# DCN-v2 cross layers on Trainium2: the first layer's second half column-tiled, both halves' remainder products in one place

## The chip, the cores and the metric

The kernel runs on one core of one Trainium2 chip. The metric is the device time of one execution in microseconds (us), as the median of several runs. PE is the matrix engine, and PEld its weight loads; DVE, ACT, POOL and SP are the vector, scalar, general-purpose and sync engines. SP and ACT also issue transfers (DMA).

## What is computed

```python
B, F, D, L = 4096, 26, 16, 6
Din = min(F * D, 1024)                 # 416
x0: (B, Din) bf16, ws: (L, Din, Din) bf16, bs: (L, Din) bf16
def reference(x0, ws, bs):
    x = x0
    for l in range(ws.shape[0]):
        x = x0 * (x @ ws[l] + bs[l]) + x
    return x
```

Six cross layers, one after the other, over 4096 rows of 416 features.

## The kernel before

The state is kept transposed: features on partitions, batch rows along the free dimension. 416 features are 3 chunks of 128 (`NK`, index k for the input features and m for the output features) and a remainder of 32 (`R`). The batch is 2 halves (`NS`, index s) of 4 groups (`NG`, index g) of 512 columns (`CW`). `XM[0]` holds x0, and `XM[1]`, `XM[2]` the running state, alternately. The 32 remainder features of the four groups stand side by side on the partitions of `XR`: group g of half s on partitions 32g to 32g+31, columns 512s on. `XRd` is a copy of `XR[0]` with the upper and lower 64 partitions exchanged; the first layer's row products for m = 1 read it, on the other two strips of the array than those for m = 0 and 2.

For each output chunk m and two groups (a "block": one half s, one pair of groups h, two banks of PSUM) PE makes:

- full products: 3 chunks k of 128 features by 512 columns for each group. In the first layer (`full` in `first_layer`, L214) a product uses the whole 128x128 array. In the later layers (`mm_full`, L181) it is cut into four, column-tiled: 32 output features each, side by side in the array.
- row products (L221 in the first layer, L187 in `mm_row`): the 32 remainder features as input, row-tiled, 32 rows of the array for each group.
- remainder products (`mm_rem`, L193 and L198): the 32 remainder features as output, column-tiled, one strip for each group; 16 instructions for a half.

ACT evicts a block from PSUM with the bias added (`ew_main`, L165), DVE multiplies by x0 (L166) and adds the state (L169). `ew_rem` does the same for a half's remainder (L173, L174, L175).

The first layer runs while x0 comes in. SP issues the transposing transfers of x0 (`load_x0t`, L76) in the order (s,g) = (0,0), (0,1), (0,2), (0,3), (1,0); then the second half's remainder columns (`load_xrem1`, L85); then (1,1), (1,2), (1,3), and after them the weights of the later layers (L72, L91) and the rows of x0 (L125). The second half's remainder comes as plain rows into `xrem`; POOL copies it to `xrig` (L134), PE transposes it (`x0_rem`, L157) and DVE copies the result from PSUM into `XR[0]` and `XRd` (L160). For the first half `xrig` is loaded directly.

`first_layer(s)` handles one half: the blocks of groups 0 and 1 for m = 0, 1, 2 (`pa`), the row products that close them and open the fourth block, then the three blocks of groups 2 and 3 (`pb`), their last row products, and then the half's remainder products into `pr`. In the first half the transposes of `x0_rem(1)` follow, into the second part of the same tile `pr`. Then the eviction of the remainder. From the second layer on (the loop over l up to LL-1) `rem_pair` makes both halves' remainder products together, once a layer, behind the first two output chunks. The last layer is done by rows (L327, L333, L336), with the results leaving from DVE's sums (L344, L355).

All PSUM tiles come from one pool of four buffers of two banks; a tile takes the buffer that was given back first, and PE waits until it was evicted. Each engine works through its instructions in order.

Of the kernel before, what the change touches and what calls it, by code (L numbers as in the profile page):

```python
# [11 lines left out]
BF16 = mybir.dt.bfloat16  # L12
FP32 = mybir.dt.float32
# [3 lines left out]
def kernel(  # L17
# [7 lines left out]
    nc = tc.nc  # L25
    B, D = x0.shape
    L = ws.shape[0]
    P = 128
# [3 lines left out]
    NS = 2  # L32
    NG = 4
    CW = 512
# [8 lines left out]
    psum = ctx.enter_context(tc.tile_pool(name="psum", bufs=4, space=bass.MemoryType.PSUM))  # L43
# [4 lines left out]
    ident = const.tile([P, P], BF16)  # L48
# [12 lines left out]
    scrR = [big.tile([P, 4, P], BF16, name=f"scrR{s}") for s in range(NS)]  # L61
    xrem = big.tile([P, 16, R], BF16)
    xrig = big.tile([P, NS, 4, P], BF16)
# [4 lines left out]
    def col0(s, g):  # L68
        return SW * s + CW * g
# [84 lines left out]

    def x0_rem(s, tpr):
        for i in range(4):
            nc.tensor.transpose(tpr[:, 128 * i:128 * i + 128], xrig[:, s, i, :], ident[:])  # L157
        for dst, src in ((slice(0, P), slice(0, P)), (slice(64, P), slice(0, 64)), (slice(0, 64), slice(64, P))):
            to = XR[0] if dst == src else XRd
            nc.vector.tensor_copy(to[dst, CW * s:CW * s + CW], tpr[src])  # L160

    def ew_main(l, s, m, h, pt, cur, nxt, pin=False):
        c0 = col0(s, 2 * h)
        t = tpool.tile([P, 2 * CW], BF16, name="t")
        nc.scalar.activation(t[:], pt[:].rearrange("p a b -> p (a b)"), ACT.Identity, bias=bM[:, m, l:l + 1], scale=1.0)  # L165
        prod = nc.vector.tensor_tensor(out=t[:], in0=t[:], in1=XM[0][:, m, c0:c0 + 2 * CW], op=ALU.mult)  # L166
        if pin:
            tc.keep_in_program_order(prod)
        nc.vector.tensor_tensor(out=nxt[:, m, c0:c0 + 2 * CW], in0=t[:], in1=cur[:, m, c0:c0 + 2 * CW], op=ALU.add)  # L169

    def ew_rem(l, s, pr, curR, nxtR):
        tr = tpool.tile([P, 2 * CW], BF16, name="t")
        nc.scalar.activation(tr[:, 0:CW], pr, ACT.Identity, bias=bR[:, l:l + 1], scale=1.0)  # L173
        nc.vector.tensor_tensor(out=tr[:, 0:CW], in0=tr[:, 0:CW], in1=XR[0][:, CW * s:CW * s + CW], op=ALU.mult)  # L174
        nc.vector.tensor_tensor(out=nxtR[:, CW * s:CW * s + CW], in0=tr[:, 0:CW], in1=curR[:, CW * s:CW * s + CW], op=ALU.add)  # L175

    def mm_full(l, s, m, g, pts, cur, first, last):
        c0 = col0(s, g)
        for k in range(NK):
            for q in range(4):  # L180
                nc.tensor.matmul(pts[g // 2][32 * q:32 * q + 32, g % 2, :], lhsT=WM[:, l, k, 128 * m + 32 * q:128 * m + 32 * q + 32],  # L181
                                 rhs=cur[:, k, c0:c0 + CW], start=(first and k == 0), stop=(last and k == NK - 1),
                                 tile_position=(0, 32 * q))
# [7 lines left out]
    def mm_rem(l, s, pr, cur, curR):  # L191
        for g in range(NG):
            nc.tensor.matmul(pr[32 * g:32 * g + 32, :], lhsT=WD[:, l, g, :], rhs=curR[:, CW * s:CW * s + CW],  # L193
                             start=True, stop=False, tile_position=(0, 32 * g))
        for k in range(NK):
            for g in range(NG):
                c0 = col0(s, g)
                nc.tensor.matmul(pr[32 * g:32 * g + 32, :], lhsT=WM[:, l, k, NK * P:D], rhs=cur[:, k, c0:c0 + CW],  # L198
                      start=False, stop=(k == NK - 1), tile_position=(0, 32 * g))
# [4 lines left out]
    def xl_dmat(s, k, nxt):  # L204
        nc.sync.dma_start_transpose(out=XLrows[:, 16 * s:16 * s + 16, 128 * k:128 * k + 128],
                                    in_=nxt[:, k, SW * s:SW * s + SW])

    def first_layer(s):
        cur, curR, nxt, nxtR = XM[0], XR[0], XM[1], XR[1]

        def full(pt, m, h, gl, after_row):
            c0 = col0(s, 2 * h + gl)
            for k in range(NK):
                nc.tensor.matmul(pt[:, gl, :], lhsT=WM[:, 0, k, 128 * m:128 * m + 128], rhs=cur[:, k, c0:c0 + CW],  # L214
                                 start=(k == 0 and not after_row), stop=(k == NK - 1 and after_row))

        def row(pt, m, h, opens):
            for gl in range(2):
                rg = 32 * ((2 * h + gl) ^ (2 if m == 1 else 0))
                src = XRd if m == 1 else curR  # L220
                nc.tensor.matmul(pt[:, gl, :], lhsT=WR[rg:rg + 32, 0, 128 * m:128 * m + 128],  # L221
                                 rhs=src[rg:rg + 32, CW * s:CW * s + CW],
                                 start=opens, stop=not opens, tile_position=(rg, 0))

        def ph(m):
            return psum.tile([P, 2, CW], FP32, tag="ps", name=f"ph{m}")

        pa = [ph(m) for m in range(NK)]
        if s == 0:
            for m in range(NK):  # L230
                full(pa[m], m, 0, 0, False)
            tp0 = psum.tile([P, CW], BF16, tag="ps", name="tpr")
            x0_rem(0, tp0[:])
            for m in range(NK):
                full(pa[m], m, 0, 1, False)
        else:
            for m in range(NK):
                for gl in range(2):
                    full(pa[m], m, 0, gl, False)
        pb = [ph(0)]  # L240
        row(pa[0], 0, 0, False)
        row(pb[0], 0, 1, True)
        row(pa[2], 2, 0, False)
        row(pa[1], 1, 0, False)
        for m in range(NK):
            ew_main(0, s, m, 0, pa[m], cur, nxt)
        for m in range(NK):
            if m:
                pb.append(ph(m))
            for gl in range(2):  # L250
                full(pb[m], m, 1, gl, m == 0)
        row(pb[1], 1, 1, False)
        row(pb[2], 2, 1, False)
        pr = psum.tile([P, 2, CW], FP32, tag="ps", name="pr")
        mm_rem(0, s, pr[:, 0, :], cur, curR)
        if s == 0:
            x0_rem(1, pr[:, 1, :].bitcast(BF16)[:, 0:CW])
        for m in range(NK):
            ew_main(0, s, m, 1, pb[m], cur, nxt, pin=(s == 0))
        ew_rem(0, s, pr[:, 0, :], curR, nxtR)  # L260

    bias_setup()
    pe_filler(1, CW)
    for s in range(NS):
        first_layer(s)

    def rem_pair(l, cur, curR, nxtR, feeds_last):
        pr2 = psum.tile([P, 2, CW], FP32, tag="ps", name="pr2")
        for s in range(NS):
            mm_rem(l, s, pr2[:, s, :], cur, curR)  # L270
        for s in range(NS):
            ew_rem(l, s, pr2[:, s, :], curR, nxtR)
            if feeds_last:
                nc.sync.dma_start_transpose(out=scrR[s][:], in_=nxtR[:, CW * s:CW * s + CW])

    def xl_rem(s):
        tc.keep_in_program_order(
# [3 lines left out]
    cur, curR = XM[1], XR[1]  # L281
    for l in range(1, LL):
        nxt, nxtR = XM[1 + (l % 2)], XR[1 + (l % 2)]
        feeds_last = (l == LL - 1)
# [10 lines left out]
        for n in range(0, len(tiles), 2):  # L295
            ta, tb = tiles[n], tiles[n + 1]
            pts[ta] = new_pts()
            for g in range(NG):
                mm_full(l, ta[0], ta[1], g, pts[ta], cur, True, False)
            mm_row(l, ta[0], ta[1], pts[ta], curR, False, True)  # L300
            pts[tb] = new_pts()
            mm_row(l, tb[0], tb[1], pts[tb], curR, True, False)
            if feeds_last and n == 4:
                xl_rem(0)
            finish(ta)
            for g in range(NG):
                mm_full(l, tb[0], tb[1], g, pts[tb], cur, False, True)
            finish(tb)
            if n == 0:
                rem_pair(l, cur, curR, nxtR, feeds_last)  # L310
        if feeds_last:
            xl_rem(1)
        cur, curR = nxt, nxtR

    l = LL
# [97 lines left out]
```

## Time and profile before

| | |
|---|---|
| median of 3 runs | 130.97 us (130.72 to 131.04) |
| the profiled execution | 130.71 us, of which the profile's span is 128.9 us |
| PE busy | 123.1 us (96% of the span), 1,690 products |
| DVE busy | 107.1 us (83%) |
| ACT busy | 86.9 us (67%) |
| POOL busy | 5.9 us (5%) |
| granted PE clock | 0.998 of full speed |

All times in the lines are us from the start of the span, and durations of single instructions on the page are ns. A line of a timeline gives start, length, engine, source line, operation, output and inputs, the shape, and how many instructions are merged in it. `128*32` stands for 128 rows and 32 columns of the array. Each product is listed at 0.38 us because its length includes the pipeline; products follow each other at shorter intervals, so starts are compared with starts. An idle stretch stands in brackets behind the instruction that ends it, with what released it. In the chain that ended last, each piece is what the next one waited for, and a piece of PE is merged from neighbouring instructions of one line.

### The profile page before, as it was taken

To read this page: it belongs to the slowest core of one execution; us is meant where nothing else is said; L and a number is where in the kernel's file an instruction comes from. 1 tells how busy PE (TensorE), PEld (TensorE's weight loads), DVE (VectorE), ACT (ScalarE), POOL (GpSimd) and SP (SyncE) were. 2 spreads that over 40 slices of the span, in tenths; PEclk is the share of its full clock that TensorE was granted. 3 is DMA by queue.
4 is the path that set the end of the run, shared out by engine and by line. 5 is a ranking of instruction groups with operands and counts; after the bars stand their busy time and mean duration, and the time that the engine had idled before them with its cause. 6 is when DMAs were issued, how large, how long until landed. Compare 5 with 4: busy or idle time off the path is not lost.

```text
span 128.9 us, 3973 instructions
## 1 busy us (share of the span) xinstructions
PE 123.1 (96%) x1690; PEld 54.9 (43%) x1690; DVE 107.1 (83%) x197; ACT 86.9 (67%) x99; POOL 5.9 (5%) x18
## 2 busy tenths in 40 slices
PE   6999999999999999999999999999999999999960
PEld 2343443354444444444444444444444445445420
DVE  1032979999999898989898989898989899898991
ACT  0426783987848577848668848668847896569670
POOL 4022200600000000000000000000000000000000
PEclk9999999999999999999999999999999999999999
DMA  3999999999990000000000000000297999995754
GB/s 106 237 203 217 170 158 260 247 328 333 336 299 11 5 0 8 0 0 5 0 5 0 5 0 5 0 5 0 42 166 164 123 219 178 187 323 188 231 179 139
DMA packets 42102, 16.37 MB, mean 127 GB/s; under 512 B 30906, under 2 KB 42084, under 8 KB 42084
## 3 DMA queue, kind: packets, MB, share of 16 engines
q1 hardware_dynamic: 39416, 15.56, 54.6%
q10 hardware_dynamic: 2668, 0.56, 2.3%
q8 instruction: 13, 0.21, 0.7%
q14 instruction: 5, 0.04, 0.1%
HBM read 6.15 MB, written 3.41 MB: 74 GB/s over the span
## 4 chain that ended last, share of the span: by engine, by line
PE 80%; DMA 8%; DVE 5%; issue 2%; SPq 1%; ACT 1%; DVEq 0%
PE pt L181 49%; PE ph L214 9%; DMA XM<-in_x_dram 8%; PE py L327 8%; PE pt L187 5%; PE pr L198 5%; DVE t L355 3%; DVE o L344 2%; PE pr L193 2%; SPq L76 1%; PE py L333 1%; PE ph L221 1%; PE py L336 1%; ACT t L354 1%; PE pr L157 0%
## 5 line engine op out<-in xcount | busy, mean ns | idle before, releaser
L181 PE MATMUL pt<-XM,WM 128*32 128x512 bf16 x1152 | 65.2, 379 | 0.0
L165 ACT ACTIVATE t<-pt,bM 128x1024 bf16<-128x1024 f32 x48 | 49.6, 1115 | 18.3 <-PE pt L187 18.3
L166 DVE TENSOR_TENSOR t<-t,XM 128x1024 bf16<-128x1024 bf16 x60 | 41.4, 690 | 5.3 <-ACT t L165 5.3
L169 DVE TENSOR_TENSOR XM<-t,XM 128x1024 bf16<-128x1024 bf16 x60 | 41.8, 696 | 3.4
L181 PEld LDWEIGHTS <-WM 128*32 128x32 bf16 x1152 | 29.7, 97 | 33.8 <-issue 5.1
L354 ACT CAST t<-py 128x416 bf16<-128x416 f32 (+1 forms) x23 | 14.8, 642 | 4.8 <-PE py L327 2.1
L327 PE MATMUL py<-WM,XM 128*128 128x416 bf16 x96 | 17.7, 340 | 0.0
L214 PE MATMUL ph<-XM,WM 128*128 128x512 bf16 x72 | 16.5, 379 | 0.1
L165 ACT ACTIVATE t<-ph,bM 128x1024 bf16<-128x1024 f32 x12 | 12.5, 1114 | 4.4 <-PE ph L221 4.4
L327 PEld LDWEIGHTS <-XM 128*128 128x128 bf16 x96 | 9.0, 98 | 8.5 <-issue 1.4
L355 DVE TENSOR_TENSOR t<-t,X0rows 128x416 bf16<-128x416 bf16 (+1 forms) x23 | 10.4, 454 | 1.2 <-ACT t L354 1.2
L214 PEld LDWEIGHTS <-WM 128*128 128x128 bf16 x72 | 6.8, 98 | 8.6 <-issue 1.3
L344 DVE TENSOR_TENSOR o<-t,XLrows 128x416 bf16<-128x416 bf16 (+1 forms) x23 | 10.3, 451 | 0.0
L173 ACT ACTIVATE t<-pr,bR 128x512 bf16<-128x512 f32 x10 | 6.4, 684 | 2.7 <-PE pr L198 2.1
L198 PE MATMUL pr<-XM,WM 128*32 128x512 bf16 x120 | 8.2, 379 | 0.0
L187 PE MATMUL pt<-XR,WR 32*128 32x512 bf16 x96 | 7.3, 379 | 0.0
L141 PE MATMUL wps<-warm 128*128 128x512 bf16 (+1 forms) x11 | 4.4, 593 | 1.2 <-DVE warm L94 1.2
L175 DVE TENSOR_TENSOR XR<-t,XR 128x512 bf16<-128x512 bf16 x10 | 4.2, 423 | 0.7
L198 PEld LDWEIGHTS <-WM 128*32 128x32 bf16 x120 | 3.2, 97 | 3.1
L106 ACT ACT_TABLE_LOAD x1 | 1.3, 1283 | 4.3 <-DMA WM<-in_ws_dram 4.3
L174 DVE TENSOR_TENSOR t<-t,XR 128x512 bf16<-128x512 bf16 x10 | 4.2, 418 | 0.0
L152 DVE CAST bM<-pb 128x18 f32<-128x18 bf16 x1 | 0.2, 177 | 4.6 <-PE pb L151 4.6
(39 smaller groups left out, 33.6 us busy)
## 6 DMA issues: line engine op xcount, KB each, us to landing
X0rows<-in_x_dram SPq DMA_DIRECT2D x4, 832.0 KB, 11.6
out_dram<-o SPq DMA_DIRECT2D x9, 208.0 KB, 2.4
WM<-in_ws_dram SPq DMA_DIRECT2D x5, 312.0 KB
out_dram<-o SPq DMA_DIRECT2D x13, 104.0 KB, 1.7
WR<-in_ws_dram SPq DMA_DIRECT2D x4, 130.0 KB, 4.1
WM<-in_ws_dram ACTq DMA_DIRECT2D x1, 312.0 KB
XM<-in_x_dram SPq DMA_TRANSPOSE x8, 4.9
xrig<-in_x_dram ACTq DMA_DIRECT2D x4, 32.0 KB, 4.1
```

The source lines that it names most:

```text
L165: nc.scalar.activation(t[:], pt[:].rearrange("p a b -> p (a b)"), ACT.Identity, bias=bM[:, m, l:l + 1], scale=1.0)
L166: prod = nc.vector.tensor_tensor(out=t[:], in0=t[:], in1=XM[0][:, m, c0:c0 + 2 * CW], op=ALU.mult)
L169: nc.vector.tensor_tensor(out=nxt[:, m, c0:c0 + 2 * CW], in0=t[:], in1=cur[:, m, c0:c0 + 2 * CW], op=ALU.add)
L173: nc.scalar.activation(tr[:, 0:CW], pr, ACT.Identity, bias=bR[:, l:l + 1], scale=1.0)
L181: nc.tensor.matmul(pts[g // 2][32 * q:32 * q + 32, g % 2, :], lhsT=WM[:, l, k, 128 * m + 32 * q:128 * m + 32 * q + 32], rhs=cur[:, k, c0:c ...
L187: nc.tensor.matmul(pts[g // 2][:, g % 2, :], lhsT=WR[32 * g:32 * g + 32, l, 128 * m:128 * m + 128], rhs=curR[32 * g:32 * g + 32, CW * s:CW ...
L198: nc.tensor.matmul(pr[32 * g:32 * g + 32, :], lhsT=WM[:, l, k, NK * P:D], rhs=cur[:, k, c0:c0 + CW], start=False, stop=(k == NK - 1), tile ...
L214: nc.tensor.matmul(pt[:, gl, :], lhsT=WM[:, 0, k, 128 * m:128 * m + 128], rhs=cur[:, k, c0:c0 + CW], start=(k == 0 and not after_row), sto ...
L327: nc.tensor.matmul(py[:, 0:D], lhsT=cur[:, k, q_cols(q, g)], rhs=WM[:, l, k, :], start=((not closes) and k == 0), stop=(closes and k == NK ...
L344: tc.keep_in_program_order(nc.vector.tensor_tensor(out=o, in0=t, in1=xl, op=ALU.add))
L354: nc.scalar.copy(tv, src)
L355: tc.keep_in_program_order(nc.vector.tensor_tensor(out=tv, in0=tv, in1=X0rows[:, b, :], op=ALU.mult))
```

## The change

In the second half of the first layer (s = 1) three things differ:

- `full` calls `mm_full`, so that the 36 full products are 144 column-tiled ones.
- `x0_rem(1)` makes 16 column-tiled transposes of 32 by 128 instead of 4 of 128 by 128, into a tile of its own (`tp1`).
- The remainder products of both halves are made by one call of `rem_pair`, behind the fourth block of the second half (its first block of groups 2 and 3), and their evictions follow there. The first half makes none, and the second half none at its end.

The function `rem_pair` is only moved up in the file, unchanged. The source lines below the edit shift by up to 17 (in the kernel after, `full` stands at L231, the row products at L238, the transposes at L157 and L161, `mm_full` at L186).

```diff
--- before.py
+++ after.py
@@ -154,7 +154,12 @@
 
     def x0_rem(s, tpr):
         for i in range(4):
-            nc.tensor.transpose(tpr[:, 128 * i:128 * i + 128], xrig[:, s, i, :], ident[:])
+            if s == 0:
+                nc.tensor.transpose(tpr[:, 128 * i:128 * i + 128], xrig[:, s, i, :], ident[:])
+                continue
+            for g in range(NG):
+                nc.tensor.transpose(tpr[32 * g:32 * g + 32, 128 * i:128 * i + 128], xrig[:, s, i, 32 * g:32 * g + 32], ident[:],
+                                    tile_position=(0, 32 * g))
         for dst, src in ((slice(0, P), slice(0, P)), (slice(64, P), slice(0, 64)), (slice(0, 64), slice(64, P))):
             to = XR[0] if dst == src else XRd
             nc.vector.tensor_copy(to[dst, CW * s:CW * s + CW], tpr[src])
@@ -205,10 +210,22 @@
         nc.sync.dma_start_transpose(out=XLrows[:, 16 * s:16 * s + 16, 128 * k:128 * k + 128],
                                     in_=nxt[:, k, SW * s:SW * s + SW])
 
+    def rem_pair(l, cur, curR, nxtR, feeds_last):
+        pr2 = psum.tile([P, 2, CW], FP32, tag="ps", name="pr2")
+        for s in range(NS):
+            mm_rem(l, s, pr2[:, s, :], cur, curR)
+        for s in range(NS):
+            ew_rem(l, s, pr2[:, s, :], curR, nxtR)
+            if feeds_last:
+                nc.sync.dma_start_transpose(out=scrR[s][:], in_=nxtR[:, CW * s:CW * s + CW])
+
     def first_layer(s):
         cur, curR, nxt, nxtR = XM[0], XR[0], XM[1], XR[1]
 
         def full(pt, m, h, gl, after_row):
+            if s == 1:
+                mm_full(0, s, m, 2 * h + gl, {h: pt}, cur, not after_row, after_row)
+                return
             c0 = col0(s, 2 * h + gl)
             for k in range(NK):
                 nc.tensor.matmul(pt[:, gl, :], lhsT=WM[:, 0, k, 128 * m:128 * m + 128], rhs=cur[:, k, c0:c0 + CW],
@@ -249,29 +266,20 @@
                 pb.append(ph(m))
             for gl in range(2):
                 full(pb[m], m, 1, gl, m == 0)
+            if s == 1 and m == 0:
+                rem_pair(0, cur, curR, nxtR, False)
         row(pb[1], 1, 1, False)
         row(pb[2], 2, 1, False)
-        pr = psum.tile([P, 2, CW], FP32, tag="ps", name="pr")
-        mm_rem(0, s, pr[:, 0, :], cur, curR)
         if s == 0:
-            x0_rem(1, pr[:, 1, :].bitcast(BF16)[:, 0:CW])
+            tp1 = psum.tile([P, CW], BF16, tag="ps", name="tpr")
+            x0_rem(1, tp1[:])
         for m in range(NK):
             ew_main(0, s, m, 1, pb[m], cur, nxt, pin=(s == 0))
-        ew_rem(0, s, pr[:, 0, :], curR, nxtR)
 
     bias_setup()
     pe_filler(1, CW)
     for s in range(NS):
         first_layer(s)
-
-    def rem_pair(l, cur, curR, nxtR, feeds_last):
-        pr2 = psum.tile([P, 2, CW], FP32, tag="ps", name="pr2")
-        for s in range(NS):
-            mm_rem(l, s, pr2[:, s, :], cur, curR)
-        for s in range(NS):
-            ew_rem(l, s, pr2[:, s, :], curR, nxtR)
-            if feeds_last:
-                nc.sync.dma_start_transpose(out=scrR[s][:], in_=nxtR[:, CW * s:CW * s + CW])
 
     def xl_rem(s):
         tc.keep_in_program_order(
```

## The prediction

> **What bounds the kernel now.** The page comes first: which engine is full, and at what clock.
>
> ```profile
> PE 123.1 (96%) x1690; PEld 54.9 (43%) x1690; DVE 107.1 (83%) x197; ACT 86.9 (67%) x99; POOL 5.9 (5%) x18
> PEclk9999999999999999999999999999999999999999
> ```
>
> PE is nearly always at work and at full clock. The chain that ended last says whether it ever waits:
>
> ```profile
> 12.10 0.04 issue
> 12.14 3.40 PE ph L214 x15
> ...
> 26.25 0.65 PE pr L198 x12
> 26.90 2.59 PE pt L181 x48
> 29.49 0.54 PE pt L187 x8
> 30.03 2.71 PE pt L181 x48
> ```
>
> From 12.14 on, when the last transposed block of the first half has landed, to 115.8, every piece of the chain is PE. So whatever moves the start of the second layer's products (L181) moves the end, unless something else gives way. PE's own timeline gives the starts around the change:
>
> ```profile
> 15.47 0.39 PE L221 MATMUL ph<-XRd,WR 32*128 32x512 bf16 x2
> ...
> 15.80 0.40 PE L193 MATMUL pr<-XR,WD 128*32 128x512 bf16 x4
> 16.02 0.82 PE L198 MATMUL pr<-XM,WM 128*32 128x512 bf16 x12
> 16.78 0.40 PE L157 MATMUL pr<-ident,xrig 128*128 128x128 bf16 x4
> ```
>
> ```profile
> 21.00 0.60 PE L221 MATMUL ph<-XR,WR 32*128 32x512 bf16 x6
> ...
> 21.54 4.06 PE L214 MATMUL ph<-XM,WM 128*128 128x512 bf16 x18
> ...
> 26.73 2.76 PE L181 MATMUL pt<-XM,WM 128*32 128x512 bf16 x48
> 29.42 0.61 PE L187 MATMUL pt<-XR,WR 32*128 32x512 bf16 x8
> ```
>
> The second half's full products start at 17.01. Call u one pass of 512 columns (one full product, or four tiled ones side by side) and s the extra time where the tiling changes. From 17.01 to 21.00 there are 18 passes and a change, 18u+s = 3.99; from 21.00 to 21.54 two and a change, 2u+s = 0.54. So u = 0.216 and s = 0.11 us. The 48 column-tiled products of L181, 12 passes, take 26.73 to 29.42: 12u+s = 2.69 again. A column-tiled pass costs PE what a full one does. Last, what feeds PE here, from POOL's and SP's timelines:
>
> ```profile
> 15.26 0.79 POOL L134 COPY xrig<-xrem 128x512 bf16<-128x512 bf16 x1 [4.76 <-DMA xrem<-in_x_dram]
> ```
>
> ```profile
> 11.45 2.68 SPq L76 DMA_TRANSPOSE XM<-in_x_dram  x1
> ```
>
> That copy feeds the second half's transposes of L157; its semaphore rises at 16.07. The transfer issued at 11.45 is the second half's second block (g=1); in the trace the last of its 16 landing events is at 17.13. Before, PE comes to the transposes at 16.78 and to that block three passes after 17.01, at 17.66: both are ready, by 0.7 and 0.5 us. The first half's four passes of remainder products, 15.80 to 16.66, are what hides them.
>
> **The change, part by part.** *Tiling.* The 36 full products become 144 column-tiled ones and the 4 transposes 16: 120 more pairs of load and product on PE (1,810 for 1,690), in the same number of passes. PE's changes of tiling between 15.80 and L181: before five (products to transposes, full to row, row to full, full to row, row to column); after, counted from the end of the row products at 15.80, four (column to row and back, twice). Gain: one s, 0.11 us.
>
> The loads: by form, the profile has
>
> ```profile
> L181 PEld LDWEIGHTS <-WM 128*32 128x32 bf16 x1152 | 29.7, 97 | 33.8 <-issue 5.1
> L214 PEld LDWEIGHTS <-WM 128*128 128x128 bf16 x72 | 6.8, 98 | 8.6 <-issue 1.3
> ```
>
> 97 and 98 ns, both beside running passes of 216: no cost for the products. The transposes have passes of only 128 columns. Full ones went 56 ns apart, 0.23 for four; no row shows column-tiled ones that short with loads of 32 columns. Bounds: 0.23 if the loads hide, 0.39 if each group of four waits out one load (4 times 97). Nearest is L157 itself, so 0.23; the rest of the sum absorbs either. [...]
>
> *The remainder products of the first half leave 15.80 to 16.66.* They go, with the second half's, behind the fourth block of the second half: 8 passes there for 4+4 before, so no work is saved, and the cover over the copy and the transfer is gone. From the end of the row products, after:
>
> - PE stands ready at 15.80; POOL's copy lets the transposes start at 16.11 (semaphore 16.07 and 0.04, as a load followed its landing at 8.33 by 0.04). They end their passes at 16.34.
> - Three passes on the block g=0 (landed 13.95): 16.98.
> - The block g=1 lands at 17.13; PE resumed 0.04 after the landing at 12.11, so here at 17.17.
> - 15 passes: 20.40. Change, two row passes, change: 21.05.
> - 6 passes of the fourth block, 8 of remainders, 12 of the last two blocks, no change of tiling between: 26u = 5.61, so 26.66.
> - Change, one row pass, change: 27.09, where L181 starts. Before it was 26.73.
>
> So +0.36 us. Without waits the same passes would bring L181 to 26.61 (-0.12: the change of tiling saved, and rounding); the waits at the copy and at the block together add 0.48.
>
> *What is moved past what.* The issue order on SP is unchanged and its transfers wait only for transfers, so the landings stay. ACT no longer has the first half's remainder eviction (0.69 us at L173) and DVE no longer its two operations of 0.42 before the second half; both come after the third block's. The next waits in line after: block g=3 lands at 21.27 and PE comes to it at 21.70. The remainder tile takes the buffer of the half's first block. ACT's row tells when that is empty:
>
> ```profile
> 21.43 4.13 ACT L165 ACTIVATE t<-ph,bM 128x1024 bf16<-128x1024 f32 x4 [2.12 <-PE ph L221]
> ```
>
> It began 0.43 after the row products at 21.00, and one eviction is 1.115 long; after, the row products are at 20.51, so the buffer is free at 22.05, and PE wants it at 22.35. Cover 0.30. The other two blocks' evictions follow 1.0 apart (23.06 and 24.06), wanted at 24.07 and 25.37. DVE needs 1.33 per block and 0.9 per remainder: the remainder rows of the second layer, wanted at 29.8, are written by about 26.9, and the last block of the first layer at about 31.8 (before 31.4), wanted not before 34. So nothing else stands in the way, and +0.36 goes to the end.
>
> The profiled execution took 130.71 in all, around a span of 128.9; it is at the lower end of the runs (130.72 to 131.04, median 130.97). I add to the median: 131.33. A measurement of this kernel can tell about 0.3%, 0.39 us, from no change, so the forecast lies just inside that edge.
>
> **Rivals.** *The waits vanish.* Block g=1 lands by 16.67 and the copy is done by 15.80; then only the tiling change is left: -0.12, 130.85. For it: transposed blocks took 4.9 us to land by the median, this one 5.7; at 4.9 it would be there at 16.36. Against: the copy alone then still holds PE to 16.98 (+0.17), and an earlier queue would also start PE earlier at 12.14, in both kernels. Chance 0.14, with 0.06 in it for a gain above 0.39 of which I see no source: PE's passes are fixed.
>
> *An instruction block falls on the transfer.* In the trace one 16 KB packet of instructions runs from 17.84 to 18.94, and of the 16 landings of block g=2 four come by 18.71 and twelve only at 19.80 to 19.93. With four times the instructions per pass PE may ask for it sooner. It decides if it starts before 17.0: block g=1 then lands up to 1.1 later, near 18.2, and the sum is +1.4: 132.4. Against: in before the packet came 0.7 after the landing at 17.13, which PE's instruction stream waits for after as well, at nearly the same count. Chance 0.10. [...]
>
> *The remainder tile waits for its buffer.* The cover of 0.30 fails if ACT starts the half's evictions later or waits for the second of them (23.06, 0.7 after 22.35). Price 0.1 to 0.7, say 0.4: +0.75, 131.7. Chance 0.10.
>
> **How the numbers follow.** The forecast has 0.66: +0.17 (the copy alone binds) to +0.6 (the landing 0.25 later than profiled). About half of it lies above 0.39, rather more since the unseen costs only add: 0.35 of 0.66. Slower: 0.35+0.10+0.10 = 0.55. Faster 0.06, same the rest, 0.39. The range leaves out the instruction block and the unseen gain: from 130.85 to 132.0, which holds both the vanished waits and most of the buffer case, and the spread of the median.
>
> **What would show it.** After: PE idle before the second half's transposes until about 16.1, released by POOL's copy; a second gap before the 13th column-tiled product of that half, released by the transfer, near 17.17; L181 of the second layer at 27.1; no gap before the remainder products; the remaining 88.9 us to 115.6 unchanged. It is wrong if L181 starts at 26.6, if the gap ends past 17.5, or if PE idles at 22.3.

## The result, and the profile after

The kernel after took 131.87 us (median of 9 runs, 131.58 to 132.99) beside 130.97 before: 0.90 us more, ratio 1.0088 (95% interval 1.0065 to 1.0110). A second job (a later set of runs of both kernels) gave 131.57 beside 130.78, 1.0060 (1.0042 to 1.0077). It is slower, and by over twice the 0.36 us forecast.

No engine that limits the kernel has more work to speak of: PE has its 120 additional pairs of load and product in 0.3 us more of busy time. POOL has 0.9 us more, 0.35 of it in the copy of L134 (1.15 us for 0.79):

```profile
PE 123.4 (95%) x1810; PEld 55.5 (43%) x1810; DVE 107.4 (83%) x197; ACT 86.9 (67%) x99; POOL 6.8 (5%) x18
```

The chain that ended last, in order of time, now leaves PE between 12 and 17 us. Before, it was PE from 12.14 on; here it runs over the remainder's transfer and POOL's copy:

```profile
9.36 1.75 SPq L76
11.11 0.04 issue
11.16 4.53 DMA xrem<-in_x_dram
...
15.80 1.16 POOL xrig L134
16.96 0.04 issue
17.00 0.41 PE tpr L161 x16
17.41 3.88 PE ph L186 x72
21.29 0.54 PE ph L238 x8
21.84 1.41 PE ph L186 x24
```

PE's timeline (the idle time before an instruction and its releaser in brackets at the end) shows the one gap:

```profile
15.63 0.39 PE L238 MATMUL ph<-XR,WR 32*128 32x512 bf16 x2
17.00 0.41 PE L161 MATMUL tpr<-ident,xrig 128*32 128x128 bf16 x16 [0.99 <-POOL xrig L134]
17.23 4.06 PE L186 MATMUL ph<-XM,WM 128*32 128x512 bf16 x72
21.23 0.60 PE L238 MATMUL ph<-XR,WR 32*128 32x512 bf16 x6
...
21.77 1.48 PE L186 MATMUL ph<-XM,WM 128*32 128x512 bf16 x24
...
27.82 2.77 PE L186 MATMUL pt<-XM,WM 128*32 128x512 bf16 x48
```

The transposes could have started at 15.95 (0.33 after the row products); they started at 17.00. The second layer starts at 27.82, 1.09 later than before; from there to the last instruction it is 102.2 us in both. Some of the 1.09 is not the change's: the last block of the first half landed at 12.25 here and 12.11 before. So from here on the time is counted from the first half's last row products (L221 before) to the second layer's first product, written D. Landing times are the last of a transfer's 16 landing events, as in the prediction. Before, D is 26.73 less 15.48, 11.25; after, 27.82 less 15.62, 12.20.

A second and a third profile of the same kernel show the gap in another shape. The third's PE:

```profile
15.74 0.39 PE L238 MATMUL ph<-XR,WR 32*128 32x512 bf16 x2
16.33 0.41 PE L161 MATMUL tpr<-ident,xrig 128*32 128x128 bf16 x16 [0.20 <-POOL xrig L134]
16.56 0.82 PE L186 MATMUL ph<-XM,WM 128*32 128x512 bf16 x12
17.78 3.42 PE L186 MATMUL ph<-XM,WM 128*32 128x512 bf16 x60 [0.40 <-DMA XM<-in_x_dram]
```

Here the copy ends early, and the 13th product waits for block g=1, exactly the two gaps that the prediction drew. (The bracket counts from the end of the listed length; by starts PE lost 17.78-16.56-0.65 = 0.57 there.)

### The profile page after: what moved, and what is told of

It is laid out like the page before. It is cut to its first block, busy times and chain, and to the rows that moved or that the text cites. A ratio compares the mean times of both kernels' runs of the same rounds, so it can differ in the third digit from the quotient of the medians.

```text
span 130.0 us, 4214 instructions
## 1 busy us (share of the span) xinstructions
PE 123.4 (95%) x1810; PEld 55.5 (43%) x1810; DVE 107.4 (83%) x197; ACT 86.9 (67%) x99; POOL 6.8 (5%) x18
## 4 chain that ended last, share of the span: by engine, by line
PE 77%; DMA 7%; DVE 5%; SPq 4%; issue 2%; POOL 1%; ACT 1%; DVEq 0%; POOLq 0%
PE pt L186 49%; PE py L335 8%; PE ph L186 6%; PE pt L192 5%; PE pr L203 5%; SPq L76 4%; DMA XM<-in_x_dram 4%; DMA xrem<-in_x_dram 3%; DVE t L363 3%; DVE o L352 2%; PE pr L198 2%; PE py L341 1%; POOL xrig L134 1%; PE py L344 1%; PE ph L238 1%
## 5 line engine op out<-in xcount | busy, mean ns | idle before, releaser
L186 PE MATMUL pt<-XM,WM 128*32 128x512 bf16 x1152 | 65.2, 379 | 0.0
L186 PEld LDWEIGHTS <-WM 128*32 128x32 bf16 x1296 | 33.4, 97 | 37.6 <-issue 5.7
L231 PE MATMUL ph<-XM,WM 128*128 128x512 bf16 x36 | 8.7, 389 | 0.1
L186 PE MATMUL ph<-XM,WM 128*32 128x512 bf16 x144 | 8.3, 379 | 0.0
L231 PEld LDWEIGHTS <-WM 128*128 128x128 bf16 x36 | 3.4, 100 | 4.6 <-issue 1.3
L203 PEld LDWEIGHTS <-WM 128*32 128x32 bf16 x120 | 3.2, 97 | 3.3
```

## The experiments

Three theories went in. P: the loss is PE's wait for POOL's copy, which the first half's remainder products used to cover. T: the transfer of block g=1 binds right behind it. C, the rival: column-tiled products cost PE more than whole-array ones.

**The move without the tiling.** In the kernel after, the branches for s = 1 are taken out of `x0_rem` and `full`; the cut in `full` is shown:

```diff
-            if s == 1:
-                mm_full(0, s, m, 2 * h + gl, {h: pt}, cur, not after_row, after_row)
-                return
```

> The kernel after without its tiling: the second half's 36 products and 4 transposes use the whole array again, only the remainder products are moved. Theory P (the move took away PE's cover over POOL's copy of the second half's remainder, and PE waits for that copy): the loss stays, with two more changes of tiling around the moved remainder products (0.22 us) on top of the kernel after: 131.9 to 132.2 us, PE idle before the transposes until POOL's copy ends. Theory C (the column-tiled products and transposes cost PE more than the whole-array ones): the loss is gone, 130.9 to 131.2 us.

Measured 131.91 us, ratio 1.0086 (1.0054 to 1.0118). The loss stays although that half's 36 full products and its transposes use the whole array, so C falls. PE's timeline has a third gap, at the fourth block's second group:

```profile
16.11 0.40 PE L158 MATMUL tpr<-ident,xrig 128*128 128x128 bf16 x4 [0.28 <-POOL xrig L134]
16.34 0.81 PE L228 MATMUL ph<-XM,WM 128*128 128x512 bf16 x3
17.44 3.40 PE L228 MATMUL ph<-XM,WM 128*128 128x512 bf16 x15 [0.29 <-DMA XM<-in_x_dram]
...
22.32 0.81 PE L228 MATMUL ph<-XM,WM 128*128 128x512 bf16 x3 [0.19 <-DMA XM<-in_x_dram]
```

By starts these are 0.34, 0.45 and 0.35 us. Block g=3 landed at 22.28; it is the transfer that the prediction named as next in line, with 0.43 of cover from a landing at 21.27.

**The tiling without the move.** The kernel before, with the two tiled branches of the change's diff and nothing else of it.

> The kernel before with only the tiling of the second half's products and transposes; the first half's remainder products stay ahead of the transposes. Theory P: the cover is back, no wait at the transposes, one change of tiling fewer than before: 130.85 us, 0.12 under the kernel before. Theory C: the loss stays, 131.7 to 132.0 us.

> The kernel before with only the tiling, once more for its times: one change of tiling saved, 0.11 to 0.13 us under the kernel before (ratio 0.999).

Measured 130.70 beside 130.83 (ratio 0.9984, 0.9968 to 1.0000), and in the second job 130.85 beside 130.83 (1.0002, 0.9987 to 1.0017). PE does not wait:

```profile
15.72 0.39 PE L229 MATMUL ph<-XR,WR 32*128 32x512 bf16 x2
16.04 0.40 PE L198 MATMUL pr<-XR,WD 128*32 128x512 bf16 x4
...
16.91 0.40 PE L161 MATMUL pr<-ident,xrig 128*32 128x128 bf16 x16
17.14 4.06 PE L186 MATMUL ph<-XM,WM 128*32 128x512 bf16 x72
...
26.87 2.76 PE L186 MATMUL pt<-XM,WM 128*32 128x512 bf16 x48
```

D is 11.15 in both of its profiles, 0.10 under the kernel before: the one change of tiling saved. In the time that is too little to tell from nothing. So no kernel here is shown to beat the kernel before; of the change, the tiling is harmless and the move is the loss.

**The remainder's transfer earlier.** In the kernel after, in SP's order:

```diff
-    load_x0t(1, 0)
     load_xrem1()
+    load_x0t(1, 0)
```

> The kernel after with one transfer earlier in SP's order: the second half's remainder rows go ahead of that half's first block instead of behind it, so POOL's copy is done some 1 to 2 us sooner. Theory P alone: PE no longer waits, 130.85 us. Theory T (as predicted: the block g=1 of the second half is next and binds as well): PE comes to it at about 16.8 and waits until its landing at 17.1 to 17.7, so 131.2 to 131.7 us, with the gap before the 13th tiled product. Theory C: no change from the kernel after, 131.9 us.

Measured 131.46, ratio 1.0044 (1.0025 to 1.0062). The copy ended at 14.30, no gap is left before the transposes, and all of the wait stands before block g=1 (landed 17.42):

```profile
15.94 0.41 PE L161 MATMUL tpr<-ident,xrig 128*32 128x128 bf16 x16
16.18 0.82 PE L186 MATMUL ph<-XM,WM 128*32 128x512 bf16 x12
17.46 3.42 PE L186 MATMUL ph<-XM,WM 128*32 128x512 bf16 x60 [0.47 <-DMA XM<-in_x_dram]
```

P alone would have brought it to 130.85. T holds: with the copy out of the way PE still waits 0.63 us by starts for the transfer alone (D is 11.79, 0.64 over the 11.15 of the tiling alone). The transposes follow the row products at once here, so their new tile `tp1` does not wait for its buffer either.

**Three passes ahead of the transposes.** In the kernel after, `x0_rem(1)` comes behind the first block's group g=0 of the second half (the part of the edit that moves it):

```diff
+            if s == 0 and m == 0:
+                early.append(psum.tile([P, 2, CW], FP32, tag="ps", name="ph0"))
+                mm_full(0, 1, 0, 0, {0: early[0]}, cur, True, False)
+                tp1 = psum.tile([P, CW], BF16, tag="ps", name="tpr")
+                x0_rem(1, tp1[:])
```

> The kernel after with the second half's first three passes (block g=0, landed at about 14) put ahead of the transposes, 0.65 us of cover over POOL's copy. Theory P alone: the loss shrinks by 0.65 us, to 131.2 to 131.3 us. Theory T: PE still starts the passes on block g=1 only at its landing, 17.1 to 17.7, so between 131.3 and 131.8 us by that landing. Theory C: as the kernel after, 131.9 us.

Measured 131.51, ratio 1.0053 (1.0036 to 1.0071), inside T's range; the lower end of the interval, 131.30, touches the 131.2 to 131.3 that P alone would give, so the profile decides. PE makes the transposes at 16.26 without a wait, stands until block g=1 (landed 17.25) at 17.30, and later waits for block g=3 as well. By starts the two waits are 0.81 and 0.41 us. The first is within the waits of the kernel after (the table below): in either order PE comes to block g=1 behind the same passes.

```profile
16.26 0.40 PE L161 MATMUL tpr<-ident,xrig 128*32 128x128 bf16 x16
17.30 3.42 PE L186 MATMUL ph<-XM,WM 128*32 128x512 bf16 x60 [0.64 <-DMA XM<-in_x_dram]
...
22.25 0.83 PE L186 MATMUL ph<-XM,WM 128*32 128x512 bf16 x12 [0.23 <-DMA XM<-in_x_dram]
```

**Cover for the transfer too.** The kernel with the earlier remainder transfer, with the passes of the first three blocks in another order (the two lines that are new):

```diff
+            for m, gl in ((0, 0), (1, 0), (0, 1), (1, 1), (2, 0), (2, 1)):
+                full(pa[m], m, 0, gl, False)
```

> The kernel with the remainder's transfer ahead (e3_xrem_first), and PE makes the passes on block g=0 of two output chunks before the first on block g=1, three passes (0.65 us) of cover over the transfer. Theory T: the gap before block g=1 goes; a shorter one comes before the second chunk, whose buffer ACT empties at about 17.2 (PE there at 16.83): 131.1 us, 0.3 under e3_xrem_first. If something else than the transfer held e3_xrem_first, 131.5 us.

Measured 131.14, ratio 1.0021 (1.0002 to 1.0041). That is the expected time, 0.32 under the kernel with the earlier remainder transfer alone, but the two were timed in different jobs and their intervals overlap. In the profile, the gap before block g=1 is gone, though it landed as late as 17.68, and the shorter one for the buffer is where it was expected, 0.39 us by starts:

```profile
16.02 0.82 PE L186 MATMUL ph<-XM,WM 128*32 128x512 bf16 x12
17.06 3.44 PE L186 MATMUL ph<-XM,WM 128*32 128x512 bf16 x60 [0.22 <-ACT t L170]
...
20.97 1.70 PE L186 MATMUL ph<-XM,WM 128*32 128x512 bf16 x24
```

The last line is 1.70 long where it is 1.48 in the kernel after: inside it PE waits 0.21 us for block g=3 (landed 21.80). So D is 11.78, as with the earlier remainder transfer alone (11.79): the wait left the place that T named, but two others came up for it, and the profiles do not show a shorter stretch. The 0.3 us is not shown to come from the edit.

**The copy made twice**, in the kernel after and in the kernel before: the line at L134 is repeated.

> The kernel after with POOL's copy of the remainder made twice (the second into the same place), 0.6 to 0.8 us more of POOL. Theory P: nothing covers it; the transposes start at about 16.8 and block g=1 at 17.7 or later, so 0.2 to 0.6 us more than the kernel after, 132.1 to 132.5 us (less than the copy is long, since the wait for the block is inside it). If the copy did not matter, 131.9 us.

> The kernel before with POOL's copy made twice. Theory P: the first half's remainder products cover the second copy too (it ends at about 16.8, when PE comes to the transposes at 16.78): 130.8 to 131.0 us, no more than 0.1 over the kernel before. If the copy bound PE in the kernel before as well, 0.6 to 0.8 us more.

After: 132.04 (1.0092, 1.0058 to 1.0127), just under the expected 132.1, and 0.47 over the kernel after of the same job, inside the expected 0.2 to 0.6. POOL's and PE's timelines show the transposes at the second copy's heels:

```profile
15.48 0.72 POOL L134 COPY xrig<-xrem 128x512 bf16<-128x512 bf16 x1 [4.82 <-DMA xrem<-in_x_dram]
16.26 0.95 POOL L135 COPY xrig<-xrem 128x512 bf16<-128x512 bf16 x1
```

```profile
17.27 0.41 PE L162 MATMUL tpr<-ident,xrig 128*32 128x128 bf16 x16 [1.21 <-POOL xrig L135]
```

Before: 131.27 (1.0034, 1.0009 to 1.0059), where at most 130.9 to 131.0 was expected, so that expectation missed. Its profiled execution was its fastest (130.49) and shows no wait: the remainder landed early, at 14.76, the copies ended at 16.50, and PE came to the transposes at 16.56. In the other profiles that leave SP's order alone it landed at 15.07 to 15.69; 0.12 and two copies of 0.61 and 0.95 later is 16.8 to 17.4. In the four profiles of kernels that keep the cover and copy once, PE came to the transposes at 16.78 to 17.23; two copies would have held it there by 0.1 to 0.3 us, an estimate from these landings and lengths. That accounts for part of the 0.49 over the kernel before of the same job; the slower executions themselves were not profiled, and the rest stays open.

**Unchanged kernels once more.**

> The kernel after, unchanged, for a second profile and more times. Theories P and T together: PE loses 0.75 to 1.3 us ahead of the 13th tiled product of the second half, shared between the gap before the transposes (until POOL's copy ends, 16.05 to 16.95 in the profiles so far) and the gap before block g=1 (landed at 17.1 to 17.7 so far); 131.6 to 132.2 us. If the long copy of the first profile was the rule, the copy alone again takes all of it; if it was an exception, the copy ends near 16.1 and the rest of the wait stands before the block.

> The kernel before, unchanged, for a second profile. Theory T: block g=1 of the second half lands more than 5.02 us (the first profile's distance, the smallest so far) behind block g=3 of the first half, at about 5.3 as in the other profiles, and PE, which comes to it 5.55 behind, still does not wait for it or for POOL's copy.

> The kernel after, unchanged, for a third profile: the distance of the two landings at 5.1 to 5.5, waits of 0.5 to 1.1 us in all ahead of the 13th tiled product, shared between POOL's copy and the transfer as each ends in this execution.

The kernel after gave 131.57 as above and 131.71 (one time); the kernel before 130.79. The numbers side by side (us; the distance is from the landing of the first half's last block to that of the second half's block g=1; "wait" is D less the 11.15 of the tiling alone, which has the same passes and changes of tiling):

| profile | copy ends | transposes | distance | 13th product | D | wait |
|---|---|---|---|---|---|---|
| before | 16.06 | 16.78 | 5.02 | 17.66 | 11.25 | |
| before, second | 16.16 | 16.89 | 5.40 | 17.77 | 11.25 | |
| after | 16.95 | 17.00 | 5.44 | 17.88 | 12.20 | 1.05 |
| after, second | 16.19 | 16.24 | 5.10 | 17.54 | 11.71 | 0.56 |
| after, third | 16.27 | 16.33 | 5.38 | 17.78 | 12.00 | 0.85 |

The kernel before does not wait in either profile, though in the second the block landed at 17.61, 0.16 before PE came to it. The last part of the expectation for the long copy is answered too: 1.15 us was the exception, the longest copy of all thirteen profiles; 0.61 is the commonest length, with others from 0.69 to 0.95.

## Why the prediction was right and where it was wrong

Right: **the work.** 18 tiled passes and a change took 17.23 to 21.23, 4.00 us beside 3.99; the 16 tiled transposes took 0.23, the lower of the two bounds; the change of tiling saved is worth 0.10 by D (forecast 0.11). The tiled loads, 97 ns in the mean beside 100 for the whole-array ones in the first profile after, cost nothing that a run shows: the tiling alone is no slower (ratios 0.9984 and 1.0002).

Right: **the mechanism.** The waits are at the two places named, released by the copy and by block g=1, and nothing behind them moves in the kernel after: no gap before the remainder products at any buffer, and 102.2 us from the second layer to the end in every profile.

Wrong: **the size of the wait**, forecast as 0.48 and measured as 0.56, 0.85 and 1.05 in three profiles, 0.82 in the mean. With the 0.10 saved that makes 0.72 by the profiles, for a forecast of 0.36. By its own sign the forecast failed too: the gap before the 13th product ended at 17.54 and 17.78 in the two profiles that have it, past 17.5. The step that failed is "the block g=1 lands at 17.13 ... so here at 17.17". It took the landing of a single execution as its place, and that execution had the shortest distance, 5.02 us (shared with one of the tiling alone): the eleven profiles that leave SP's order alone run from 5.02 to 5.44, with a mean of 5.28. That mean alone adds 0.26 and makes +0.62. Before, nothing depended on it, since PE came 5.55 behind; the change made PE come 4.56 behind (without waits), where all of the spread is paid. (The five profiles of kernels with the cover have 5.02 to 5.42, 5.22 in the mean, the six without it 5.10 to 5.44, 5.33 in the mean; that the move itself adds a little to the distance is not excluded.) The prediction allowed "the landing 0.25 later than profiled" as the far end of its likeliest case; it was the middle. That the measured 131.87 still lies under the 132.0 of its range is luck: the room up there was left mostly for the wait on the remainder tile's buffer, which did not occur.

Wrong, smaller: **POOL's copy**, put at 0.79 long and done at 16.05. In the first profile after, the remainder landed 0.54 later than in the first profile before, and the copy took 1.15; the wait at the transposes was 1.05 there, for a forecast of 0.31, and 0.15 and 0.27 in the other two. It matters less than it looks: without any wait for the copy, PE would have come to block g=1 at 16.83 in that profile and stood there until 17.72, 0.89 us, so the long copy added 0.16 of the 1.05.

Of the rivals, the waits did not vanish, and PE did not wait at 22.35 for the remainder tile's buffer. The block of instructions came at 19.57, 18.24 and 18.51 in the three profiles after, beside 17.84 before, never ahead of block g=1. The prediction's 0.43 of cover at block g=3 also rested on one landing (21.27); others were up to 22.60, and three of the experiments waited for it.

The three profiles' 0.72 stands against 0.79 to 0.90 in the medians. Part of that is where PE's stretch starts: the row products stood at 15.48 and 15.58 in the two profiles before and at 15.62 to 15.77 in the three after; in the other kernels they stand between 15.23 and 16.03, so this looks like spread. Why the landings vary by 0.4 us from one execution to the next was not settled.

## What to carry to other kernels

Work that sits between an engine and its next input is cover even when it is not late: before moving it, list every input that arrives within its length, not only the first. Where a change uses up such slack, the arrival time in one profile is one draw from a spread (here 5.02 to 5.44 us after the landing of the first half's last block); take several profiles, or several like transfers, and price the mean of the wait, which only counts lateness. Separating the two halves of the change showed at once that the part with four times the instructions was free (130.70 and 130.85 us beside 130.83 for the kernel before) and the reordering was not (131.91).

## What the runs showed of the hardware

POOL's copy and DVE's adds and multiplies stretched each other here, and the one that started second took longer. In the second profile before, POOL's copy began first; its length is 0.61 and DVE's add, 0.69 elsewhere, took 1.01. In the first profile after, DVE began 0.01 ahead, kept its 0.69, and the copy took 1.15:

```profile
15.55 0.61 POOL L134 COPY xrig<-xrem 128x512 bf16<-128x512 bf16 x1 [4.97 <-DMA xrem<-in_x_dram]
```

```profile
15.69 1.01 DVE L169 TENSOR_TENSOR XM<-t,XM 128x1024 bf16<-128x1024 bf16 x1
```

```profile
15.80 1.15 POOL L134 COPY xrig<-xrem 128x512 bf16<-128x512 bf16 x1 [5.09 <-DMA xrem<-in_x_dram]
```

```profile
15.79 0.69 DVE L174 TENSOR_TENSOR XM<-t,XM 128x1024 bf16<-128x1024 bf16 x1
```

In the first profile before, DVE's multiply had 0.32 us left when the copy began, and the copy took 0.79; in the first profile after, DVE's add had 0.68 left, and the copy took 1.15. That is 0.36 more of overlap and 0.36 more of copy: by these two, over that stretch the copy stood still rather than ran slower. In the thirteen profiles, each of the nine copies that took longer than 0.61 ended 0.47 us after the DVE operation that had begun before it (16.05 for 15.58 in the first profile before, 16.95 for 16.48 in the first after), and each DVE operation that began during a copy ended 0.54 to 0.55 us after the copy's end (16.60 for 16.05 in the first profile before, 16.70 for 16.16 in the second). So a transfer that lands some hundredths of a microsecond earlier or later decided here whether POOL's copy was 0.61 or 1.15 us long: in the third profile after, it began at 15.66, 0.02 ahead of the add, and took 0.61; in the first, at 15.80, 0.01 behind the add, and took 1.15, and PE stood behind it.
